# A gated linear recurrence feeding a multiplicative feed-forward layer: the decay parameter read as two rows, fewer turns on TensorE, and a new order of the steps

## The chip, the cores and the metric

The kernel runs on one core of a Trainium2 chip. The metric is device time in microseconds (us). The core has a matrix engine (TensorE, PE in the profile), a vector engine (VectorE, DVE), a scalar engine (ScalarE, ACT), a general engine (GpSimd, POOL) and a queue engine (SyncE, SP) that here only issues DMA transfers. Each engine works through its own list of instructions in order and waits on semaphores for the others.

## The reference, cut to what matters

```python
x, r_gate, i_gate: (4, 5824, 256)   a_param: (256,)
w1, w2: (256, 1024)   w3: (1024, 1024)   w_out: (1024, 256)

a_base = sigmoid(a_param)
log_a = 8 * sigmoid(r_gate) * log(clip(a_base, 1e-6, 1 - 1e-6))
a_t = exp(log_a)
x_gated = sqrt(maximum(1 - a_t * a_t, 1e-6)) * sigmoid(i_gate) * x
for t in range(5824):                    # each batch starts from h = 0
    h = a_t[:, t] * h + x_gated[:, t]
    y[:, t] = h
tokens = y.reshape(23296, 256)
out = (((tokens @ w1) * (tokens @ w2)) @ w3) @ w_out
```

## The kernel before

The 23,296 tokens are cut into 46 chunks, the first of 256 tokens and 45 of 512. Since nothing nonlinear stands between `w3` and `w_out`, their product `wp` is formed once at the start (the "fold": `Ft` turns a piece of w3, `Fc` copies it, `Fm` multiplies it with w_out, `Fe` evacuates it to `wp_sb`). Each chunk then goes through two halves.

*The recurrence.* `r`, `i`, `x` load the chunk with tokens on the partitions (L118). `R` and `I` are the tanh of the gates on ScalarE (L126, L136). `p` adds one to tanh(i) and `t` multiplies it with x, which gives `u` (L142, L146), mostly on GpSimd. `V` turns tanh(r) and `U` turns u so that channels lie on the partitions: either TensorE does it (`turn_pe`, L162, eight 128x128 transposes into PSUM) or a DMA transpose issued from SP (`turn_dma`, L174). The sets `TURN_R` and `TURN_U` say which chunks TensorE turns. A chunk that is in both sets is loaded with longer rows (`long_rows`, L109). `d` is the exponential that gives a_t, with the decay rate `la4` as scale and bias (L181), `s` its square, `q` the root on ScalarE, `g` the gated product on VectorE (L202), `h` the scan over time on VectorE, in two halves of 128 channels (L214), and `y` the cast to bf16 (L229).

*The feed-forward half.* `a` and `b` are the two up-projections, each in four groups of four matmuls into a tile of PSUM (L240; three such tiles); `c` copies the result of `a` to SBUF as bf16 (L256), `m` multiplies it with the result of `b` on VectorE (L262), `D` is the down-projection with `wp`, eight matmuls for 128 tokens (L269; two tiles of PSUM, which the turns share), `e` evacuates two of these (L281) and `o` stores 256 tokens (L294).

The decay rate is prepared once: `A0` and `A2` are short VectorE instructions on a tile of 128x2, and `A1` is an exponential on ScalarE between them (L349 to L366). `W` are matmuls on the identity whose result nobody reads; they stand ahead of the first work of TensorE.

The order isn't left to a scheduler. The program is recorded by walking a long string, `ORDER`, in which each word is one step with its chunk and part (`a12.3` is group 3 of `a` of chunk 12). Every engine's list has its instructions in the order of that string. Sets such as `DV_COPY`, `DV_EVAC`, `DV_SQUARE` and `DV_CAST` give the steps that VectorE takes; copies and evacuations not named there go to ScalarE, squares and casts not named there to GpSimd. `L` and `C` with a weight's name load a piece of a weight in f32 into a staging buffer and cast it to bf16. ScalarE has tanh and exp in one table and sqrt in another, so that each change between `R`, `I`, `d` and `q` brings a load of a table; copies work with either.

```python
nc.scalar.dma_start(out=la4, in_=a_param.rearrange("(cb p) -> p cb", p=P))
for word in ORDER.split():
    name, args = re.fullmatch(r"([LC]w[123o]\.|A\d\.|[A-Za-z]+)([\d.]*)", word).groups()
    steps[name](*(int(v) for v in args.split(".") if v))
```

Of the kernel before, what the change touches and what calls it, by code (L numbers as in the profile page):

```python
# [22 lines left out]
def kernel(  # L23
# [12 lines left out]
    nc = tc.nc  # L36
# [31 lines left out]
    la4 = consts.tile([P, NCB], F32, tag="la4")  # L68
    zz, zd, zt = (consts.tile([P, NCB], F32, name=tag, tag=tag) for tag in ("zz", "zd", "zt"))
# [9 lines left out]
    TURN_R = {0, 1, 2, 3, 4, 5, 7, 8, 13}  # L79
    TURN_U = {0, 1, 2, 3, 5, 8, 9}  # L80
    DV_TIMES = {0, 1, 2, 8}
    DV_PLUS = set()
    DV_HALF = set()
    DV_SQUARE = {(0, 0), (0, 1), (1, 0), (1, 1), (5, 0), (6, 0), (7, 1), (9, 1), (11, 0), (12, 0), (14, 0), (15, 1),
        (20, 1), (24, 1), (27, 0), (29, 0), (36, 0), (37, 0), (38, 0), (41, 0)}
    DV_CAST = {0, 20, 28, 37, 39, 40, 42, 45}
    DV_COPY = {(0, 3), (1, 1), (1, 3), (2, 1), (3, 2), (7, 2), (8, 0), (8, 1), (10, 0), (11, 1), (13, 0), (14, 0),
        (14, 2), (15, 3), (18, 1), (18, 3), (19, 3), (20, 3), (21, 3), (22, 3), (23, 1), (25, 0), (25, 2), (28, 1), (33,
        1), (33, 2), (36, 3), (40, 2), (41, 2), (41, 3), (44, 0), (45, 0)}
    DV_EVAC = {(0, 0), (1, 1), (2, 0), (2, 1), (3, 0), (4, 0), (4, 1), (5, 0), (6, 1), (7, 1), (8, 1), (9, 1), (10,  # L90
        0), (17, 0), (18, 1), (19, 0), (19, 1), (22, 0), (23, 1), (27, 0), (27, 1), (28, 1), (30, 0), (31, 0), (33, 1),
        (34, 1), (35, 0), (35, 1), (41, 1), (42, 0), (42, 1)}
    FOLD_ACT = {('c', 7), ('e', 0), ('e', 1), ('e', 4), ('e', 6), ('e', 7)}
    W_ACT = {('w2', 0), ('w3', 1), ('w3', 2), ('w3', 3)}
    W_DVE = {('w3', 0)}
    STAGE = {'w1': ['a', 'a'], 'w2': ['nrm', 'nrm'], 'wo': ['a', 'nrm'], 'w3': ['a', 'nrm', 'a', 'nrm', 'a', 'nrm',
        'a', 'nrm']}
    WARM = [30, 30, 24]
# [47 lines left out]
    def times(c, half):  # L146
# [168 lines left out]
    def load_w(nm, i):  # L315
        T["wf", nm, i] = held.tile([P, NCB, CT], F32, name="wf", tag=STAGE[nm][i])
        nc.sync.dma_start(out=staged(nm, i), in_=piece(nm, i)[0])
# [30 lines left out]

    def rates_abs():  # L349
        nc.vector.scalar_tensor_tensor(out=zz, in0=la4, scalar=-1.0, in1=la4, op0=ALU.mult, op1=ALU.min)  # L350
        nc.vector.tensor_scalar(la4, la4, -4.0, 0.0, op0=ALU.mult, op1=ALU.max)
# [22 lines left out]
    def last(c):  # L374
# [17 lines left out]
        "W": warm, "E": cast_ident, "A0.": rates_abs, "A1.": rates_exp, "A2.": rates,  # L392
# [3 lines left out]
        A0. r1 r0 i0 Lw3.0 x0 i1 A1. E R1 R0 x1 V0 V1 Lw1.1 Cw1.1 I0 A2. d0.0 d0.1 d1.0 d1.1 r2 Lw1.0 Lw2.0 Lw2.1 W1  # L396
        I1 s0.0 Cw3.0 s0.1 t0.1 s1.0 s1.1 W0 U0 i2 Cw1.0 q0 t1.1 g0 h0.0 q1 R2 U1 Lw3.1 h0.1 y0 W2 a0.2 g1 h1.0 c0.2
        V2 x2 h1.1 Lwo.1 Cw2.1 Cw2.0 Lwo.0 Ft0 a0.0 r4 a0.1 d2.0 c0.0 Lw3.2 c0.1 r3 b0.0 b0.1 s2.0 m0.0 m0.1 I2 d2.1
        Lw3.5 y1 Fc0 b0.2 b0.3 m0.2 s2.1 Lw3.4 a0.3 c0.3 m0.3 Cw3.1 Cwo.1 a1.2 Ft1 q2 a1.0 t2.1 Cwo.0 U2 i3 a1.1 c1.2
        b1.0 Fc1 c1.0 g2 c1.1 h2.0 R4 h2.1 m1.0 Lw3.3 Fm1 Fm0 Fe1 Fe0 y2 i4 b1.1 Cw3.5 r6 V4 b1.2 m1.1 m1.2 R3 V3 d4.0  # L400
        d4.1 a1.3 Ft5 d3.0 b1.3 a2.0 d3.1 Cw3.2 Fc5 x3 Ft2 c1.3 s4.0 Cw3.4 s4.1 I3 Lw3.6 Lw3.7 r5 s3.0 x4 s3.1 c2.0
# [127 lines left out]
```

## Time and profile before

| | |
|---|---|
| time, median of 3 runs | 521.2 us (521.09 to 521.59) |
| the profiled execution's own time | 520.88 us |
| its span, first to last instruction | 519.1 us |
| DMA: moved, mean rate | 123.28 MB, 237 GB/s |
| DMA transposes of u, of tanh(r) | 39, 37 |
| copies `c` of full chunks on ScalarE, on VectorE | 149 (mean 1012 ns), 31 (1214 ns) |
| evacuations `e` of 512 columns on ScalarE, on VectorE | 58 (mean 585 ns), 31 (680 ns) |
| table loads on ScalarE | 40 of 1283 ns |

The busy share of an engine is an average over the whole span. The matmuls overlap each other, so the mean duration of one (379 ns for 512 columns, 273 ns for 256) is more than the time from one start to the next (216 and 109 ns in an unbroken stream). ScalarE and VectorE overlap consecutive instructions a little as well. A wait is shown before the instruction that ended it, with what released it.

### The profile page before, as it was taken

What the parts mean: (1) busy time and instruction counts of PE and PEld (TensorE: products, weight loads), DVE (VectorE), ACT (ScalarE), POOL (GpSimd) and SP (SyncE); (2) the same over time, 40 slices, a digit from 0 to 9 for tenths busy, and PEclk for the clock granted to TensorE, in tenths of its full rate; (3) what the DMA queues carried; (4) which work ended last, traced back from release to release, by engine and by line L of the source; (5) the groups of instructions that cost most, each with busy time, mean ns of one, the idle gap of its engine ahead of it and who ended that gap; (6) DMA issues with size and microseconds to landing.
All of it is one profiled execution on the core that took longest, in us unless ns stands there. A gap on an engine that the chain in (4) does not pass through costs nothing.

```text
span 519.1 us, 8770 instructions
## 1 busy us (share of the span) xinstructions
PE 498.2 (96%) x3203; PEld 309.0 (60%) x3260; DVE 478.3 (92%) x456; ACT 429.7 (83%) x493; POOL 299.9 (58%) x251
## 2 busy tenths in 40 slices
PE   4799999999999999999999999999989999999997
PEld 4567656656565666566665655666556565666555
DVE  4999999999999999899999899999998998999973
ACT  6999998998898988999987997988977797766432
POOL 0668755786828674876566765756357746634000
PEclk9999999999999999999999999999999999999999
DMA  8999979899999786999989969988967988342113
GB/s 298 403 411 292 347 239 273 257 280 278 331 308 227 204 237 200 283 250 289 259 225 297 249 207 218 295 249 239 240 170 222 252 225 214 101 123 81 63 54 109
DMA packets 174604, 123.28 MB, mean 237 GB/s; under 512 B 84448, under 2 KB 170208, under 8 KB 174560
## 3 DMA queue, kind: packets, MB, share of 16 engines
q1 hardware_dynamic: 174288, 122.71, 83.8%
q8 instruction: 25, 0.41, 0.3%
q14 instruction: 19, 0.16, 0.1%
q10 hardware_dynamic: 272, 0.00, 0.0%
HBM read 78.91 MB, written 23.86 MB: 198 GB/s over the span
## 4 chain that ended last, share of the span: by engine, by line
PE 76%; DVE 16%; issue 5%; ACT 1%; DMA 1%; POOL 0%; DVEq 0%; ACTq 0%; POOLq 0%
PE pb L246 25%; PE po L277 24%; PE pa L246 23%; DVE g_t L266 6%; DVE h_t L225 4%; DVE sa L252 1%; PE pw L342 1%; DVE nrm L210 1%; PE ptr L167 1%; DMA la<-in_a_param_dram 1%; PE warm L238 1%; DVE nrm L195 1%; DVE nrm L207 1%; PE ptw L331 1%; DVE ot L252 1%
## 5 line engine op out<-in xcount | busy, mean ns | idle before, releaser
L246 PEld LDWEIGHTS <-w_sb 128*128 128x128 bf16 x1472 | 143.0, 98 | 150.8 <-issue 10.8
L266 DVE TENSOR_TENSOR g_t<-sa,pb 128x1024 bf16<-128x1024 bf16 (+1 forms) x184 | 215.9, 1199 | 17.4 <-PE pb L246 12.0
L254 ACT CAST sa<-pa 128x1024 bf16<-128x1024 f32 (+1 forms) x152 | 149.5, 1004 | 52.4 <-PE pa L246 47.2
L246 PE MATMUL pa<-y_t,w_sb 128*128 128x512 bf16 (+1 forms) x706 | 177.5, 377 | 5.0 <-DVE g_t L266 1.8
L246 PE MATMUL pb<-y_t,w_sb 128*128 128x512 bf16 (+1 forms) x709 | 177.9, 376 | 4.5 <-DVE sa L252 1.3
L277 PE MATMUL po<-wp_sb,g_t 128*128 128x256 bf16 x1456 | 179.4, 273 | 0.4
L277 PEld LDWEIGHTS <-g_t 128*128 128x128 bf16 x1456 | 142.3, 98 | 42.5
L225 DVE TENSOR_TENSOR_SCAN h_t<-a_t,h_t,nrm 128x512 f32<-128x512 f32 (+3 forms) x90 | 117.5, 1331 | 1.2
L160 POOL TENSOR_TENSOR u_t<-th_i,x_t 128x512 bf16<-128x512 f32 x84 | 113.8, 1373 | 1.6 <-DMA ut<-u_t 0.5
L233 POOL CAST y_t<-h_t 128x1024 bf16<-128x1024 f32 x38 | 44.5, 1170 | 118.1 <-DVE h_t L225 101.6
L195 POOL TENSOR_TENSOR nrm<-a_t 128x512 f32<-128x512 f32 x72 | 85.8, 1205 | 18.2 <-ACT a_t L188 18.1
L144 POOL TENSOR_SCALAR th_i<-th_i 128x1024 f32<-128x1024 f32 x42 | 48.7, 1163 | 30.7 <-ACT th_i L139 30.7
L188 ACT ACTIVATE a_t<-rt,la 128x512 f32<-128x512 bf16 x74 | 59.1, 818 | 3.0 <-DMA rt<-th_r 1.9
L139 ACT ACTIVATE th_i<-i_t 128x1024 f32<-128x1024 f32 (+1 forms) x46 | 48.3, 1051 | 7.1 <-DMA i_t<-in_i_gate_dram 4.2
L210 DVE SCALAR_TENSOR_TENSOR nrm<-nrm,ut 128x1024 f32<-128x1024 f32 x39 | 52.7, 1354 | 0.0
L254 ACT COPY ot<-po 128x512 f32<-128x512 f32 (+1 forms) x60 | 34.7, 578 | 17.0 <-PE po L277 16.2
L199 ACT ACTIVATE nrm<-nrm 128x1024 f32<-128x1024 f32 (+1 forms) x46 | 46.9, 1047 | 0.3
L252 DVE CAST sa<-pa 128x1024 bf16<-128x1024 f32 (+1 forms) x32 | 38.3, 1197 | 5.5 <-PE pa L246 5.4
L132 ACT ACTIVATE th_r<-r_t 128x1024 bf16<-128x1024 f32 x37 | 39.2, 1060 | 0.1
L199 ACT ACT_TABLE_LOAD x20 | 25.7, 1283 | 1.5 <-DVE nrm L195 1.1
L252 DVE COPY ot<-po 128x512 f32<-128x512 f32 (+1 forms) x33 | 21.9, 665 | 4.0 <-PE po L277 4.0
L195 DVE TENSOR_TENSOR nrm<-a_t 128x512 f32<-128x512 f32 (+1 forms) x20 | 18.2, 920 | 0.9 <-ACT a_t L188 0.9
(51 smaller groups left out, 155.0 us busy)
## 6 DMA issues: line engine op xcount, KB each, us to landing
r_t<-in_r_gate_dram SPq DMA_DIRECT2D x45, 512.0 KB, 5.5
i_t<-in_i_gate_dram SPq DMA_DIRECT2D x45, 512.0 KB, 5.2
x_t<-in_x_dram SPq DMA_DIRECT2D x45, 512.0 KB, 5.5
out_dram<-ot SPq DMA_DIRECT2D x89, 256.0 KB, 3.6
wf<-in_moe_w_dram SPq DMA_DIRECT2D x12, 512.0 KB, 8.9
wf<-in_moe_w_out_dram SPq DMA_DIRECT2D x2, 512.0 KB, 11.4
ut<-u_t SPq DMA_TRANSPOSE x39, 5.1
rt<-th_r SPq DMA_TRANSPOSE x37, 4.5
```

Source lines behind the costliest of these rows:

```text
L144: (nc.vector if c in DV_PLUS else nc.gpsimd).tensor_scalar(t, t, 1.0, 1.0, op0=ALU.add, op1=ALU.mult)
L160: (nc.vector if (c, half) in DV_HALF else nc.gpsimd).tensor_mul(out=u, in0=t, in1=xt)
L188: nc.scalar.activation(out=a, in_=pr, func=AF.Exp, scale=la4[:, cb:cb + 1], bias=la4[:, cb:cb + 1])
L195: eng.tensor_mul(out=T["n", c][:, cb, :w], in0=T["a", c][:, cb, :w], in1=T["a", c][:, cb, :w])
L199: nc.scalar.activation(out=T["n", c][:, :, :w], in_=T["n", c][:, :, :w], func=AF.Sqrt, scale=-1.0, bias=1.0)
L210: nc.vector.scalar_tensor_tensor(out=T["n", c][:, :, :w], in0=T["n", c][:, :, :w], scalar=1e-3, in1=T["pu", c][:, :, :w], op0=ALU.max, op1 ...
L225: nc.vector.tensor_tensor_scan(T["h", c][:, cb, lo:hi], T["a", c][:, cb, lo:hi], T["n", c][:, cb, lo:hi], init, ALU.mult, ALU.add)
L246: nc.tensor.matmul(out=pp[:, q, :w], lhsT=w_sb[:, cb, m * P:(m + 1) * P], rhs=T["y", c][:, cb, :w], start=(cb == 0), stop=(cb == NCB - 1))
L252: nc.vector.tensor_copy(out=dst, in_=src_ps)
L254: nc.scalar.copy(out=dst, in_=src_ps)
L266: nc.vector.tensor_mul(out=T["g", c][:, 2 * mp:2 * mp + 2, :w], in0=T["sa", c, mp][:, :, :w], in1=T["pb", c, mp][:, :, :w])
L277: nc.tensor.matmul(out=po, lhsT=T["g", c][:, k, j * P:(j + 1) * P], rhs=wp_sb[:, k, :], start=(k == 0), stop=(k == KD - 1), skip_group_che ...
```

## The change

The decay parameter is loaded as two rows of 128 values instead of 128 rows of two values. A new step, `A3`, turns it on TensorE into PSUM, and `A0` copies it to `la4` first. The sets that assign steps to engines are replaced, `times` works on one 128-channel half at a time for a fused chunk that TensorE doesn't turn (chunk 8), and `ORDER` is replaced as a whole. `CASTING` is empty, so the new branch in `load_w` does nothing.

```diff
+    la_rows = consts.tile([NCB, P], F32, tag="la_rows")
...
-    TURN_R = {0, 1, 2, 3, 4, 5, 7, 8, 13}
-    TURN_U = {0, 1, 2, 3, 5, 8, 9}
+    TURN_R = {0, 1, 2, 3, 4, 9, 16}
+    TURN_U = {0, 1, 2}
     DV_TIMES = {0, 1, 2, 8}
-    DV_PLUS = set()
-    DV_HALF = set()
-    DV_SQUARE = {(0, 0), (0, 1), (1, 0), (1, 1), (5, 0), (6, 0), (7, 1), (9, 1), (11, 0), (12, 0), (14, 0), (15, 1),
-        (20, 1), (24, 1), (27, 0), (29, 0), (36, 0), (37, 0), (38, 0), (41, 0)}
-    DV_CAST = {0, 20, 28, 37, 39, 40, 42, 45}
-    DV_COPY = {(0, 3), (1, 1), (1, 3), (2, 1), (3, 2), (7, 2), (8, 0), (8, 1), (10, 0), (11, 1), (13, 0), (14, 0),
...
-    DV_EVAC = {(0, 0), (1, 1), (2, 0), (2, 1), (3, 0), (4, 0), (4, 1), (5, 0), (6, 1), (7, 1), (8, 1), (9, 1), (10,
...
+    DV_PLUS = {6, 10}
+    DV_HALF = {(3, 0), (4, 0), (6, 1), (7, 0), (10, 1), (12, 0), (13, 0)}
+    DV_SQUARE = {(0, 0), (0, 1), (1, 1), (4, 0), (5, 0), (7, 0), (10, 1), (13, 0)}
+    DV_CAST = {1, 4, 9, 11}
+    DV_COPY = {(0, 2), (2, 0), (3, 2), (3, 3), (4, 0), (4, 1), (6, 1), (8, 0)}
+    DV_EVAC = {(9, 0), (9, 1)}
+    FOLD_ACT = {('c', 6), ('e', 1), ('e', 2), ('e', 3), ('e', 5), ('e', 6), ('e', 7)}
+    W_ACT = {('w2', 0), ('w2', 1), ('w3', 4)}
+    W_DVE = {('w1', 0), ('w3', 1)}
...
+    def rates_turn():
+        pt = psum.tile([P, 2, CT], F32, name="pr_la", tag="pab")
+        nc.tensor.matmul(out=pt[:, 0, :NCB], lhsT=la_rows, rhs=ident_f[:NCB, :NCB], is_transpose=True,
+                         start=True, stop=True)
+        T["la"] = pt[:, 0, :NCB]
+
     def rates_abs():
+        nc.vector.tensor_copy(out=la4, in_=T["la"])
...
     ORDER = """
-        A0. r1 r0 i0 Lw3.0 x0 i1 A1. E R1 R0 x1 V0 V1 Lw1.1 Cw1.1 I0 A2. d0.0 d0.1 d1.0 d1.1 r2 Lw1.0 Lw2.0 Lw2.1 W1
-        I1 s0.0 Cw3.0 s0.1 t0.1 s1.0 s1.1 W0 U0 i2 Cw1.0 q0 t1.1 g0 h0.0 q1 R2 U1 Lw3.1 h0.1 y0 W2 a0.2 g1 h1.0 c0.2
...
-        e44.1 D45.1 o44.1 e45.0 o45.0 D45.2 e45.1 o45.1 D45.3 e45.2 o45.2 e45.3 o45.3
+        r1 E A3. A0. A1. A2. R1 r0 R0 V1 d1.0 d1.1 i0 V0 x0 s1.0 I0 i1 W0 Lw1.0 t0.1 s1.1 W2 d0.0 d0.1 x1 I1 Cw1.0
+        s0.0 s0.1 q0 t1.1 q1 Lw1.1 r2 Cw1.1 R2 Lw2.1 Lw2.0 W1 U0 g0 h0.0 h0.1 y0 U1 Lw3.1 i2 Cw2.1 a0.0 a0.3 a0.1 V2
...
+        e44.0 e44.1 o44.0 D45.0 e45.0 o44.1 D45.1 e45.1 o45.1 o45.0 D45.2 D45.3 e45.2 e45.3 o45.3 o45.2
         """
 
-    nc.scalar.dma_start(out=la4, in_=a_param.rearrange("(cb p) -> p cb", p=P))
+    nc.scalar.dma_start(out=la_rows, in_=a_param.rearrange("(cb p) -> cb p", p=P))
```

## The prediction

> **What bounds the kernel now.** I first read busy shares and the chain that ended last.
>
> ```profile
> PE 498.2 (96%) x3203; PEld 309.0 (60%) x3260; DVE 478.3 (92%) x456; ACT 429.7 (83%) x493; POOL 299.9 (58%) x251
> PE 76%; DVE 16%; issue 5%; ACT 1%; DMA 1%; POOL 0%; DVEq 0%; ACTq 0%; POOLq 0%
> ```
>
> TensorE (PE) has 96% and carries 76% of the chain; VectorE (DVE), the next busiest, carries 16%. So PE's instruction stream sets the end, and VectorE interrupts it. The question is where PE isn't working. The table by stages, cut at the first up-projection (17.4 us) and at the first down-projection (50.7 us), answers:
>
> ```profile
> 0.00:17.40 17.40, 8.15 (x109) 8.01 (x110) 9.83 (x27) 11.98 (x15) 3.21 (x8) 1.00 0.88 327
> 17.40:50.70 33.30, 31.55 (x268) 21.63 (x274) 31.96 (x38) 32.56 (x40) 24.38 (x22) 1.00 1.07 371
> 50.70:150.00 99.30, 98.12 (x631) 60.61 (x641) 96.99 (x94) 92.02 (x104) 67.89 (x57) 1.00 0.99 288
> 150.00:300.00 150.00, 148.85 (x904) 89.74 (x920) 143.56 (x129) 136.63 (x157) 100.00 (x83) 1.00 0.95 249
> 300.00:450.00 150.00, 145.95 (x882) 87.69 (x898) 140.68 (x123) 123.70 (x143) 89.42 (x72) 1.00 0.85 223
> 450.00:519.10 69.10, 65.56 (x418) 41.28 (x422) 55.32 (x50) 32.85 (x39) 14.98 (x12) 1.00 0.28 85
> ```
>
> Columns: length, then busy time of PE, PEld, DVE, ACT, POOL, granted clock, DMA share, GB/s. From 17.4 to 450 us PE is idle for 1.75 + 1.18 + 1.15 + 4.05 = 8.1 us. Up to 150 us ScalarE (ACT), VectorE and the DMA engines are all nearly full too. After the last matmul (515.9 us) come 3.2 us of copy, store and closing. An edit therefore pays by taking instructions out of PE's stream, by starting it earlier, or from those 8.1 us.
>
> The timeline shows what holds the start:
>
> ```profile
> 0.73 0.45 ACTq L497 DMA_DIRECT2D la<-in_a_param_dram  x1
> 5.67 0.16 DVE L350 SCALAR_TENSOR_TENSOR zz<-la 128x2 f32<-128x2 f32 x1 [5.67 <-DMA la<-in_a_param_dram]
> 5.97 1.56 ACT L130 ACTIVATE th_r<-r_t 128x1024 bf16<-128x1024 f32 x2
> 8.84 4.86 PE L238 MATMUL warm<-ident 128*128 128x128 bf16 x60
> 13.53 0.83 PE L167 MATMUL ptr<-ident,u_t 128*128 128x128 bf16 x12
> 17.37 0.60 PE L246 MATMUL pa<-y_t,w_sb 128*128 128x256 bf16 x4 [1.67 <-DVE y_t L233]
> ```
>
> The decay parameter lands 4.9 us after its issue; ScalarE's exponential stands before its first tanh and waits for it. But the turn of u at 13.53 stands behind 60 warm-up matmuls, so two things hold the first `a`.
>
> **What the Trainium skill says.** "DMA: Bandwidth & Descriptors", Specifications, puts full rate at transfers of 512 B or more. The old load is 256 packets of 4 B (trace: first at 2.83 us, last at 4.88, landed 5.64); the new one is 2 rows of 512 B. "TensorE: Matmul & The Clock Gate", Back-to-back issue gap, gives N/2.4 + 2.5 ns warm: 56 ns for 128 columns. The trace agrees: eight turns take 0.61 us with a 0.219 us last one, (0.61 - 0.219)/7 = 0.056. "ScalarE: Activation LUTs", What ACT_TABLE_LOAD costs, has 1.28 us and a drain of 1.38 for each switch; here the next instruction starts 1.294 us after the load (load at 11.66, Sqrt at 12.95), so I use 1.294. "SBUF — State Buffer", SBUF: two separate sides, says that VectorE and GpSimd lock a shared port: here VectorE's gated product averages 1.354 us with both inputs in SBUF against 1.207 for the one of its shape that reads u from PSUM.
>
> **The change part by part.**
>
> *Turns.* TURN_R goes from 9 chunks to 7, TURN_U from 7 to 3: 6 turns of 8 transposes leave PE, all after the first `a`: 48 x 0.056 = -2.7 us of PE's stream. Nothing hides these, since PE is the bound. The turn of the parameter adds one matmul before PE has other work; behind its wait stand only the turns of chunk 1, which need the later r tile. The six become DMA transposes: 1,024 packets of 256 B at 24 ns on 16 engines = 1.5 us of DMA each, and about 1.4 us of SyncE's (SP's) time to issue. Chunks 3, 5 and 8 also lose the long-row loading. A DMA turn waits on SP for GpSimd's product, and behind it stand the next loads of r, i and x, which ScalarE's tanh needs. This costs nothing while u lands before its use; the rival prices the other case.
>
> *Start.* Two rows should land about 3.6 us (first old packet 2.83 plus the old 0.76 from last packet to landing). Transpose, copy and exponential then end near 4.7. The first r tile has landed by then (0.74 + the shortest r landing, 4.0), so the first tanh moves from 5.97 to about 4.8: -1.2 us on ScalarE. The new order puts all 84 warm-up matmuls before the turn of chunk 0's u, not 60. PE starts near 5.9 instead of 7.58, but 24 more at 0.06 us give 1.4 us of the 1.7 back. I take -0.4 for the first `a`, with -1.2 and +0.9 as bounds: the first if ScalarE's lead decides how soon the folds end, the second if u of chunk 3, now a DMA transpose behind 16 loads and all 14 weight pieces, is late for `a3`, which stands before the first `D` now. For u3: 30 transfers x 1.36 + its own 1.5, + 1.8 start + 2 landing = 46.1 us; product, scan and cast follow in 4.7 (50.8), then three groups of `a3` (2.6), where the old kernel began `D` at 50.7.
>
> *Copies and evacuations.* 24 copies and 29 evacuations move from VectorE to ScalarE. ScalarE gains 24 x 0.905 + 29 x 0.466 = +35.2 us (start to start; alone 1.012 and 0.585), but the order has 32 table loads instead of 40: -10.4. Sum near 455 us, 88% of the span. Per chunk: copies 3.6, evacuations 0.9, two tanh 1.9, two exponentials 1.4, a root 0.95, tables 0.9, or 9.7 us against PE's 32 x 0.216 + 32 x 0.109 = 10.4. It still fits beneath PE. VectorE loses 24 x 1.13 + 29 x 0.60 = 44.5 us, and 12 squares (7) and four casts (2.5) go to GpSimd (POOL); seven half-products and two additions come back (about +6). It drops to near 430, GpSimd rises to some 310. Cost at nothing: PE hides it. If it doesn't, the copy of `a` queued behind a root and its table load is what PE meets.
>
> *Order.* The trace of before can't show the new one's stalls. Bounds: -4 (half of the 8.1 us go, as VectorE's share of the chain does) and +6 (below). I take 0: VectorE has more room after 150 us, the middle of the first 100 us has less.
>
> *Tail.* The last two stores are swapped: o45.3, which waits for ScalarE's last copy, stands before o45.2 in SP's queue, so another issue follows it: +0.35 us.
>
> Sum: -2.7 - 0.4 + 0 + 0.35 = -2.75. The profiled execution took 520.88 us (span 519.10 and 1.78 around it), 0.3 below the median: 518.1 there, **518.4** as a median.
>
> **Rivals.**
>
> *Late u (slower).* Place: chunks 5 to 8. Up to U8 the new order issues 39 loads and 14 weight pieces (53 x 1.36 us, 512 KB at the 385 GB/s of loads alone), 12 transposes (1.5) and 6 stores (0.7): 94 us of DMA, against 34, 14, 7 and 5 at the same step before (79 us). From 1.8 us on and with 2.5 us to land, u8 is there at 98.6; product, scan and cast make y8 at 103.3. PE's work before `a8` (58 groups of up-projection at 0.865, 23 `D` at 0.87, folds and turns 12.8) sums to 83.0; from 17.0 and with 2.3 us of idle it arrives at 102.3. So the margin is about -1 even if DMA never pauses. For it: the old u7 comes out by this sum at 79.4, its issue was at 77.3. Against it: transposes may overlap loads (packet times run above the share 1.0), worth 3 to 4 us. Each pause of SP, which waits in order, adds its length to PE. It decides once pauses exceed about 3 us; with 5 to 8 us of them the stall is 4 to 6: 523.5.
>
> *Stalls fall too.* VectorE carries 16% of the chain and loses a tenth of its work; the idle stage 300 to 450 us holds chain pieces of VectorE. Half of the 8.1 us gone, less a little: 515.3. Against it: PE's waits are short and scattered, and each copy that leaves VectorE joins ScalarE's queue.
>
> *Exchange.* The turns' 2.7 us leave PE and come back as waits of 2 to 3 us at `a3` to `a8`: 521.0, no change.
>
> That the new load lands no earlier than the old is small: the first `a` stays and the result is 518.8, inside the first case.
>
> **How the numbers follow.** Likeliest, 0.48; stalls fall too 0.12; exchange 0.14; late u 0.26. The likeliest's own range is 516.5 to 520.3. For eight in ten the range takes most of late u and of the falling stalls: 515.3 to 524.0. What a measurement of this kernel can tell from no change is about 0.2%, 1.04 us. Faster: the second case and nearly all of the first (0.46) = 0.58. Same: exchange and the rest = 0.16. Slower: late u = 0.26.
>
> **What would show it.** Right: 120 - 48 = 72 `ptr` matmuls, first tanh near 4.8 us, first `pa` near 17, 32 table loads, ScalarE near 455 us, PE idle near 8 us after the start. Wrong: first `D` after 52 us, a gap of PE at chunk 5 to 8 released by u's product or scan, or ScalarE the owner of a good part of the chain. If PE's idle time past 50 us doubles, the forecast is wrong by as much.

## The result: no change that can be told, with a stream on TensorE that is 2.7 us shorter

| | before | changed |
|---|---|---|
| time, median | 521.22 us (521.09 to 521.59, 4 runs) | 521.68 us (520.63 to 522.32, 4 runs) |
| ratio, 95% interval | | 1.0006 [0.9985, 1.0026] |
| the profiled execution, its span | 520.88, 519.1 us | 522.25, 520.5 us |

The forecast was 518.4 us. The busy shares and the chain that ended last, after the change:

```profile
PE 498.5 (96%) x3157; PEld 308.1 (59%) x3213; DVE 437.3 (84%) x395; ACT 454.1 (87%) x538; POOL 310.3 (60%) x258
...
PE 71%; DVE 9%; ACT 9%; issue 5%; DMA 5%; SPq 1%; DVEq 0%; ACTq 0%
```

The work moved as planned: VectorE lost 41 us, ScalarE gained 24, GpSimd 10. But PE's share of the chain fell from 76% to 71%, and ScalarE and DMA transfers, 1% each before, carry 9 and 5%. The stages, with the columns of the earlier table (length, busy PE, PEld, DVE, ACT, POOL, granted clock, DMA share, GB/s):

```profile
0.00:17.40 17.40, 10.11 (x120) 9.82 (x121) 10.20 (x28) 13.17 (x17) 3.39 (x9) 1.00 0.90 336
17.40:50.70 33.30, 29.84 (x238) 20.34 (x241) 32.52 (x37) 30.93 (x37) 21.55 (x19) 0.95 1.01 341
50.70:150.00 99.30, 95.50 (x583) 56.82 (x593) 94.44 (x86) 93.98 (x114) 58.66 (x47) 1.00 1.01 281
150.00:300.00 150.00, 146.81 (x899) 89.30 (x914) 129.85 (x105) 139.28 (x165) 105.63 (x85) 1.00 0.97 261
300.00:450.00 150.00, 149.10 (x900) 89.48 (x915) 122.73 (x103) 137.59 (x161) 99.85 (x83) 1.00 0.89 226
450.00:520.50 70.50, 67.09 (x429) 42.37 (x433) 47.54 (x40) 39.17 (x49) 21.24 (x18) 1.00 0.29 96
```

Three rows are to be compared with those of before. From 50.7 to 150 us PE is idle for 3.8 us instead of 1.2, and VectorE is hardly relieved there: 94.4 us instead of 97.0. From 150 to 300 us VectorE has 14 us less to do, and PE is still idle for 3.2 us instead of 1.15. From 300 to 450 us VectorE has 18 us less, and PE is idle for 0.9 us instead of 4.05. So the change gained time only in the last of these stages, and lost it in the two ahead of it; less work on VectorE alone doesn't decide.

Busy time is a rough measure of PE, since its ends are modelled. A sharper one is PE's *lag*: the time at which a down-projection starts, less the PE work that stands ahead of it in the kernel's list (0.864 us for a group of `a` or `b`, 0.872 for a `D` or an `Fm`, 0.446 for a turn or an `Ft`, from the unbroken streams, and half of it for the groups and turns of the short chunk; warm-ups and the turns of the first two chunks count as nothing). Lag grows only where PE waits or runs slowly. It is my own sum from the trace and the list of steps:

| kernel (profiled execution) | PE work | lag at D1.0 (some 50 us) | D12.1 (170) | D23.1 (286) | last D |
|---|---|---|---|---|---|
| before | 489.1 | 20.2 | 21.9 | 22.6 | 26.7 |
| changed | 486.4 | 22.1 | 27.4 | 30.4 | 30.9 |

The account of the profiled executions closes: 2.7 us less work, +1.9 of lag at D1.0, +3.6 from there to D12.1, +2.3 to D23.1, -3.6 from D23.1 to the end, -0.1 behind the last `D`: +1.4 us, and the two executions differ by 522.25 - 520.88 = 1.37.

*The start* went better than forecast for ScalarE and for the first `a`. From the timeline of the changed kernel:

```profile
0.73 0.53 ACTq L510 DMA_DIRECT2D la_rows<-in_a_param_dram  x1
2.22 0.23 PE L357 MATMUL pr_la<-ident_f,la_rows 2*128 2x2 f32 x1 [2.22 <-DMA la_rows<-in_a_param_dram]
4.08 1.57 ACT L127 ACTIVATE th_r<-r_t 128x1024 bf16<-128x1024 f32 x2 [1.00 <-DMA r_t<-in_r_gate_dram]
16.25 1.69 PE L246 MATMUL pa<-y_t,w_sb 128*128 128x256 bf16 x12 [2.33 <-POOL y_t L233]
```

The two rows land 1.5 us after their issue instead of 4.9. The first tanh now waits for its own r tile (4.08 instead of 5.97), and the first `a` comes at 16.25 instead of 17.37. But the first `D` comes at 54.3 instead of 50.7. Of these 3.6 us, 1.7 are more PE work ahead of it in the new order. The other 1.9, and the 1.1 us that the first `a` had won, went in part to more waits between the first `a` and the first `D`, and for the greater part to the clock that was granted to PE right after its wait for the first `a`:

```profile
17.00:18.00 1.00, 1.00 (x10) 0.83 (x9) 1.00 (x2) 1.00 (x2) 0.00 (x0) 0.68 1.03 418
18.00:19.00 1.00, 1.00 (x10) 0.84 (x8) 1.00 (x1) 1.00 (x3) 0.00 (x0) 0.50 1.01 405
19.00:20.00 1.00, 1.00 (x7) 0.67 (x6) 0.97 (x3) 1.00 (x3) 0.00 (x0) 0.50 1.03 382
20.00:21.00 1.00, 1.00 (x7) 0.74 (x6) 1.00 (x3) 1.00 (x3) 0.58 (x1) 0.61 1.10 418
```

The third column from the right is the clock: half speed for some 3.4 us, which costs 1.7.

*From 50 to 132 us* PE's waits are short and many. From its timeline in that stretch:

```profile
64.17 0.62 PE L167 MATMUL ptr<-ident,th_r 128*128 128x128 bf16 x8 [1.04 <-ACT th_r L127]
86.13 0.82 PE L246 MATMUL pa<-y_t,w_sb 128*128 128x512 bf16 x3 [0.49 <-DVE g_t L266]
87.26 1.02 PE L246 MATMUL pa<-y_t,w_sb 128*128 128x512 bf16 x4 [0.30 <-DVE g_t L266]
98.68 1.90 PE L246 MATMUL pa<-y_t,w_sb 128*128 128x512 bf16 x8 [0.18 <-POOL y_t L233]
119.59 1.04 PE L246 MATMUL pa<-y_t,w_sb 128*128 128x512 bf16 x4 [0.40 <-DVE y_t L233]
```

Each bracket holds the wait and what ended it: ScalarE once, VectorE's products and casts, GpSimd's cast. No single one is large. Behind them stand further waits; between 53 and 132 us the chain of waits of the changed kernel names PE for 12% only (three lines), and DMA transfers of x (9.1%) for the first time:

```profile
by line: issue 19.4%; DVE g_t L266 16.4%; ACT sa L254 10.2%; DMA x_t<-in_x_dram 9.1%; PE pa L246 6.3%; DVE sa L252 5.9%; ACT ot L254 3.8%; ACT a_t L188 3.6%; PE po L277 3.3%; ACT th_r L129 3.3%; DVE nrm L210 2.9%; PE pb L246 2.2%; SPq L118 
```

In the same stretch of the kernel before, three PE lines alone carried 41%:

```profile
by line: DVE g_t L266 20.9%; PE po L277 17.9%; PE pb L246 12.9%; issue 12.7%; PE pa L246 10.5%; DVE h_t L225 8.7%; DVE nrm L195 4.4%; DVE sa L252 4.3%; DVE nrm L207 3.0%; PE ptr L167 1.7%; DVE ot L252 1.7%; DVE nrm L210 1.5%; DVEq L252 0.1%
```

*From 170 to 289 us* (D12.1 to D23.1) the lag grows by 3.0 us, and two waits for ScalarE's copies of `a`, near 272 and 279 us, hold 2.0 of them. At the second, the copy stands behind a table load and a root:

```profile
275.98 1.28 ACT L199 ACT_TABLE_LOAD   x1
277.27 1.06 ACT L199 ACTIVATE nrm<-nrm 128x1024 f32<-128x1024 f32 x1
278.24 0.99 ACT L254 CAST sa<-pa 128x1024 bf16<-128x1024 f32 x1
279.28 1.02 PE L246 MATMUL pb<-y_t,w_sb 128*128 128x512 bf16 x4 [1.24 <-ACT sa L254]
```

No experiment below takes these two up.

### The profile page after: what moved, and what is told of

It is laid out like the page before. It is cut to its first block, busy times and chain, and to the rows that moved or that the text cites. A ratio compares the mean times of both kernels' runs of the same rounds, so it can differ in the third digit from the quotient of the medians.

```text
span 520.5 us, 8667 instructions
## 1 busy us (share of the span) xinstructions
PE 498.5 (96%) x3157; PEld 308.1 (59%) x3213; DVE 437.3 (84%) x395; ACT 454.1 (87%) x538; POOL 310.3 (60%) x258
## 4 chain that ended last, share of the span: by engine, by line
PE 71%; DVE 9%; ACT 9%; issue 5%; DMA 5%; SPq 1%; DVEq 0%; ACTq 0%
PE po L277 23%; PE pb L246 22%; PE pa L246 22%; DVE g_t L266 4%; ACT sa L254 3%; DMA rt<-th_r 3%; DMA x_t<-in_x_dram 1%; PE warm L238 1%; PE pw L348 1%; ACT th_r L129 1%; DVE sa L252 1%; ACT ot L254 1%; DVE h_t L225 1%; DVE nrm L210 1%; ACT nrm L199 1%
## 5 line engine op out<-in xcount | busy, mean ns | idle before, releaser
L254 ACT CAST sa<-pa 128x1024 bf16<-128x1024 f32 (+1 forms) x176 | 173.4, 1005 | 38.9 <-PE pa L246 33.0
L233 POOL CAST y_t<-h_t 128x1024 bf16<-128x1024 f32 (+1 forms) x42 | 49.3, 1174 | 124.6 <-DVE h_t L225 118.7
L225 DVE TENSOR_TENSOR_SCAN h_t<-a_t,h_t,nrm 128x512 f32<-128x512 f32 (+3 forms) x90 | 121.0, 1373 | 1.5
L195 POOL TENSOR_TENSOR nrm<-a_t 128x512 f32<-128x512 f32 x84 | 96.6, 1167 | 23.3 <-ACT a_t L188 23.3
L210 DVE SCALAR_TENSOR_TENSOR nrm<-nrm,ut 128x1024 f32<-128x1024 f32 x43 | 60.7, 1413 | 6.0 <-DMA ut<-u_t 2.5
L188 ACT ACTIVATE a_t<-rt,la 128x512 f32<-128x512 bf16 x78 | 62.5, 820 | 2.5 <-DMA rt<-th_r 2.4
L141 POOL TENSOR_SCALAR th_i<-th_i 128x1024 f32<-128x1024 f32 x40 | 45.7, 1144 | 28.6 <-ACT th_i L136 28.4
L254 ACT COPY ot<-po 128x512 f32<-128x512 f32 (+1 forms) x89 | 51.6, 584 | 11.5 <-PE po L277 11.0
L199 ACT ACT_TABLE_LOAD x16 | 20.5, 1283 | 0.3
L188 ACT ACTIVATE a_t<-ptr,la 128x512 f32<-128x512 bf16 (+1 forms) x14 | 9.9, 751 | 1.4 <-PE ptr L167 1.4
L252 DVE CAST sa<-pa 128x1024 bf16<-128x1024 f32 (+1 forms) x8 | 9.2, 1148 | 1.4 <-PE pa L246 1.4
L157 DVE SCALAR_TENSOR_TENSOR u_t<-th_i,x_t 128x512 bf16<-128x512 f32 (+1 forms) x5 | 6.0, 1217 | 3.2 <-ACT th_i L136 3.0
```

The lines of the kernel that those rows point to most:

```text
L188: nc.scalar.activation(out=a, in_=pr, func=AF.Exp, scale=la4[:, cb:cb + 1], bias=la4[:, cb:cb + 1])
L195: eng.tensor_mul(out=T["n", c][:, cb, :w], in0=T["a", c][:, cb, :w], in1=T["a", c][:, cb, :w])
L199: nc.scalar.activation(out=T["n", c][:, :, :w], in_=T["n", c][:, :, :w], func=AF.Sqrt, scale=-1.0, bias=1.0)
L210: nc.vector.scalar_tensor_tensor(out=T["n", c][:, :, :w], in0=T["n", c][:, :, :w], scalar=1e-3, in1=T["pu", c][:, :, :w], op0=ALU.max, op1 ...
L225: nc.vector.tensor_tensor_scan(T["h", c][:, cb, lo:hi], T["a", c][:, cb, lo:hi], T["n", c][:, cb, lo:hi], init, ALU.mult, ALU.add)
L233: eng.tensor_copy(out=T["y", c][:, :, :w], in_=T["h", c][:, :, :w])
```

## The experiments

My theory after the result: the rows gain what was forecast or more, the new assignments gain after 300 us, and the turns' 2.7 us were exchanged for waits between 50 and 300 us, because PE isn't what that stage waits for in the new order. Rivals: one part of the change is bad by itself (the rows, the DMA turns, the copies); the DMA engines or SP's queue are full; VectorE or a few misplaced steps hold PE. Ratios are to the kernel before, measured beside each run on the same chip (medians there 521.1 to 521.7 us).

### One part at a time in the old order

**Rows alone** (`b_rows`): the old order and sets, with the parameter as rows.

```diff
-        A0. r1 r0 i0 Lw3.0 x0 i1 A1. E R1 R0
+        E A3. A0. r1 r0 i0 Lw3.0 x0 i1 A1. R1 R0
-    nc.scalar.dma_start(out=la4, in_=a_param.rearrange("(cb p) -> p cb", p=P))
+    nc.scalar.dma_start(out=la_rows, in_=a_param.rearrange("(cb p) -> cb p", p=P))
```

> The kernel before, with the decay parameter read as two rows and turned on TensorE, and nothing else (the identity's cast and the new step stand first in the order). If the wait for the parameter is what holds the start: first tanh near 4.1 us instead of 5.97, first up-projection near 16.3 instead of 17.4, time 520.2 (-1.0). If the warm-up matmuls ahead of the turn of u hold it: first tanh near 4.1 but first up-projection within 0.4 us of before, time 520.8 to 521.3.

Measured: 519.99 us, ratio 0.9967 [0.9946, 0.9988]. The lag at D1.0 is 18.3 instead of 20.2; at the last `D` it is still 1.0 lower (25.7). The first `a` comes at 15.84 us instead of 17.37. The load of the parameter did hold the start, and this part gains 1.3 us.

**DMA turns alone** (`b_turns`): the new `TURN` sets in the old order, each new DMA turn issued behind the step that produces its input, and the product of chunk 8 in two halves as in the change.

```diff
-    TURN_R = {0, 1, 2, 3, 4, 5, 7, 8, 13}
-    TURN_U = {0, 1, 2, 3, 5, 8, 9}
+    TURN_R = {0, 1, 2, 3, 4, 9, 16}
+    TURN_U = {0, 1, 2}
-        e1.1 s6.0 c4.0 b4.0 s6.1 U5 s7.1
+        U5 e1.1 s6.0 c4.0 b4.0 s6.1 s7.1
```

> The kernel before with the new sets of turns alone (48 transposes fewer on TensorE, six more DMA transposes, chunks 3, 5 and 8 without long rows); the words of the turns that move to DMA stand directly after their producers. If late u eats the gain: TensorE's lag behind its own work grows by 3 to 6 us between 50 and 150 us (1.6 before), time 521.5 to 525. If the turns are harmless and the new order is at fault: that growth stays under 2.5 us and the time is 518.5 to 519.5.

Measured: 549.19 us, ratio 1.0515 [1.0475, 1.0555], far outside both forecasts. The waits between 75 and 125 us show why. First SP's own queue, then ScalarE (waited for, us in total, times, longest):

```profile
SPq L180 <- ACT th_i L139: 11.3, 1, 11.3
SPq L180 <- DVE u_t L160: 7.2, 1, 7.2
```

```profile
ACT th_i L139 <- DMA i_t<-in_i_gate_dram: 6.7, 1, 6.7
```

L180 is the DMA turn. SP waits in order, so a turn that can't start holds every load behind it. The wait of 7.2 us, to 97.7 us, is U8's for its product; the load of i10 goes out after it, and ScalarE waits 6.7 us for that tile. The wait of 11.3 us, to 120.4 us, is V13's. Its input is done at 115.8 us; the rest of the wait is for one of the two `rt` tiles, the one that V11 filled, and the last instruction that reads that tile (`d11.1`) ends at 120.35 us. PE's lag grows by 27 us from D1.0 to D8.0 (157 us); some 8.5 of them are a clock of 0.50 behind PE's waits, for 17 us in all. My placement, not the turn, is what this prices: it shows only that a DMA turn cannot be put where I put it.

**Copies and evacuations alone** (`b_copies`): the new `DV_COPY` and `DV_EVAC` in the old order.

> The kernel before with the new sets for the copies and evacuations alone (24 copies and 29 evacuations to ScalarE), the order unchanged. With 40 table loads ScalarE gets 35 us more and is near 465 us busy. If ScalarE's load is what costs the middle of the changed kernel: 524 or more, with lag growing by more than 6 us from 50 to 300 us (2.3 before). If VectorE was the source of the stalls from 300 to 425 us: growth there falls from 4.1 to under 1.5 us and the time is 518 to 520.

Measured: 548.75 us, ratio 1.0513 [1.0487, 1.0539]. The lag grows from 22.4 us at D1.0 to 47.2 at D23.1, so the first case came in, and by far more than it asked for. ScalarE is busy for 465 us, 85% of the span, so it isn't full. From 100 to 350 us VectorE waits for ScalarE's copies; in the kernel before no such line is among the ten largest waits of that stretch:

```profile
DVE g_t L262 <- ACT sa L250: 27.4, 13, 5.4
```

My reading, which no run tests further, is that the copies stand behind other ScalarE steps in a list that was written for fewer. Neither piece gains anything alone, in the places that I gave them in the old order: sets and order are made for each other, and a sum of parts, as I made it, has no parts to add.

### Single suspects in the new order

**The first wait of PE** (`a_warm`): 30 of the 84 warm-ups moved behind U1, into the 2.3 us in which PE waited for the first `a`.

> The changed kernel with one word moved: the second group of 30 warm-up matmuls stands after the turn of chunk 1's u, directly before the first up-projection. If the idle stretch of 2.3 us before the first up-projection lets the granted clock fall to half for about 3 us: clock 1.00 throughout, all runs at 519.3 to 520.3 instead of 520.6 to 522.3 (median -1.5 to -2). If the clock is chance and the start is bound by the recurrence: first up-projection within 0.3 us of 16.25 and the median within 0.5 us of 521.7.

Measured: ratio 1.0005 [0.9993, 1.0016], 521.83 us of 20 runs. In the profile the clock stays at 1.00 and the lag at D1.0 falls from 22.1 to 20.4, and it ends at 29.7. The median is no lower than the 521.68 of the changed kernel's four runs, so the half clock isn't what made the result. With the same rows and the full clock, the first `a` comes at 15.59 us in this order and at 15.84 in the old one (`b_rows`), yet the lag at D1.0 is 20.4 here and 18.3 there. So the new order loses some 2 us already between the first `a` and the first `D`. The later runs are edits of this kernel.

**The rows undone** (`a_la`): the parameter loaded as before, `A3` taken out.

> The changed kernel with the warm-up group moved and the decay parameter loaded as before, 256 packets of 4 bytes, no turn. If the two rows' gain is real in this order too: first tanh near 6.0 instead of 4.1 us, lag at the first down-projection 21.5 to 22.5 instead of 20.4, time +1.2 to +2. If something later takes it up: time within 0.4.

Measured: 524.12 us, ratio 1.0044 [1.003, 1.0058], lag at D1.0 +2.6. The rows are worth about 2 us in the new order (2.3 by the medians, 524.12 - 521.83; 2.0 by the ratios). They aren't the loss.

**Four turns back on PE** (`a_turns`): U3, U8, U9 and V8 just ahead of their use.

```diff
-    TURN_R = {0, 1, 2, 3, 4, 9, 16}
-    TURN_U = {0, 1, 2}
+    TURN_R = {0, 1, 2, 3, 4, 8, 9, 16}
+    TURN_U = {0, 1, 2, 3, 8, 9}
```

> The changed kernel with the warm-up group moved, and four turns back on TensorE: u of chunks 3, 8 and 9 and tanh(r) of chunk 8 (chunks 3 and 8 load long rows again; chunk 8's u is one VectorE instruction again). TensorE's own work +1.8 us. If late u or the DMA load is what costs the middle: the lag's growth from 50 to 150 us falls from 5.7 to under 3, and the time is 520 or less. If VectorE and ScalarE are what is short there: growth stays over 4.5 and the time is 522.5 to 524.

Measured: 530.59 us, ratio 1.0172 [1.015, 1.0194]. Turns at 0.446 us each explain 1.8 of the 8.8 us that it is above `a_warm`. Another 3.8 us stand in the lag at D1.0 already (24.2 instead of 20.4). A step of 4.3 us in the lag, at 120 us, is the largest; ahead of that the chain runs from U8's turn (109.9 us) over gated product, scans and products on VectorE to the `pa` matmuls at 115.8; 1.7 of the 4.3 us are a clock of 0.50 from 116 to 119.4 us. Where a turn stands in PE's list decides when VectorE may go on. A price of the turns doesn't come out of this run.

**Chunk 8's product** (`a_t8`): x8 loaded ahead of x9, and the product of chunk 8, which stood ahead of three products of `m` on VectorE, moved behind them.

> The changed kernel with the warm-up group moved, and two words moved more: x of chunk 8 is loaded before x of chunk 9, and chunk 8's u on VectorE stands after the products of chunk 5 instead of ahead of them. If VectorE's wait at the head of its queue (for x, then 2.1 us of u in two halves) holds TensorE near 86 us: the step of +0.93 us of lag there goes, growth from 50 to 150 us falls to about 4.5, time -0.5 to -1. If the stretch is bound by VectorE's sum of work, the step comes back within 20 us and the time is unchanged within 0.3.

**VectorE's extra steps back on GpSimd** (`a_pool`): `DV_PLUS` and `DV_HALF` emptied.

> The changed kernel with the warm-up group moved, and the seven half-products and two additions of i that the change gave VectorE given back to GpSimd (about 8 us less on VectorE, 11 more on GpSimd, all before 130 us). If VectorE, 94% busy between 50 and 150 us, is the limit there: growth falls from 5.7 to under 4, time -1.5 to -2.5. If ScalarE or the loads are: growth within 1 of 5.7; if GpSimd makes u late: growth over 7.

**V9 later** (`a_v9`): the turn that waited for ScalarE at 62 us (64 in the changed kernel), moved behind D2.0 and a3.3.

> The kernel a_warm with one step moved: TensorE turns tanh(r) of chunk 9 (V9) after D2.0 and a3.3 instead of ahead of them, where it waited 0.8 us for ScalarE at 62 us. Theory (the stalls of the changed order between 50 and 150 us are single steps placed ahead of their producers, and each can be taken out by itself): the step of 1.0 us in PE's lag at 62 us goes, the lag at D5.0 is 23.0 instead of 23.9, and the time falls by about 0.9 from a_warm's 521.8. Rival (PE runs behind what ScalarE and VectorE finish, so a wait that is taken away returns at the next dependent step): the lag at D5.0 stays within 0.4 of 23.9 and the time within 0.4 of 521.8.

Measured: `a_t8` 523.86 us, 1.0044 [1.0023, 1.0066]; `a_pool` 523.24, 1.0034 [1.0018, 1.005]; `a_v9` 522.23, 1.0014 [0.9994, 1.0033]. In `a_t8` the step of 0.9 us in the lag at 86 us is gone, and 4.2 us come by 93 and 2.1 more by 98 us. PE's timeline shows of what:

```profile
85.06 1.04 PE L277 MATMUL po<-wp_sb,g_t 128*128 128x256 bf16 x8
...
88.67 1.02 PE L246 MATMUL pb<-y_t,w_sb 128*128 128x512 bf16 x4 [1.71 <-DVE sa L252]
91.11 1.86 PE L246 MATMUL pb<-y_t,w_sb 128*128 128x512 bf16 x4 [1.41 <-ACT sa L254]
92.77 1.91 PE L277 MATMUL po<-wp_sb,g_t 128*128 128x256 bf16 x8
```

Two waits for copies of `a` (`sa`), 3.1 us together, and behind them the same eight `po` matmuls take 1.91 us instead of 1.04: the granted clock is 0.50 from 90.2 to 97 us, which adds some 3 us to the work that PE does in it. In `a_v9` the step at 62 us is gone, 0.9 come at 74, and the lag at D5.0 is 24.4 against 23.9. So these two waits, taken away, came back at later steps. VectorE with 2.1 us less to do between 50.7 and 150 us (91.4 us, `a_pool`) doesn't help either: the lag grows by 5.2 us from D1.0 to D12.1 instead of 5.7, and it starts 1.7 higher. Neither of the two steps is the cause by itself. VectorE's sum of work doesn't look like the limit, but `a_pool` gave that work to GpSimd, which also feeds PE, so the run doesn't rule it out.

**Fewer transfers** (`a_nostore`): the stores of chunks 0 to 7 left out.

> The kernel a_warm without the stores of chunks 0 to 7, so that part of the output is not written: about 3.9 MB, some 10 us less of DMA work between 50 and 150 us, where the DMA share is 1.00. If the transfers are what PE waits for in the first 150 us (ScalarE and VectorE waiting for late r, i and x, and these for the DMA engines), the lag grows by less than 3 us from D1.0 to D12.1 instead of 5.7, and the time falls to 518 to 519.5. If the waits come from the order in which ScalarE, VectorE and PE do the steps that depend on each other, the growth stays above 4.5 and the time within 0.7 us of 521.8.

Measured: 520.63 us, ratio 0.9977 [0.9962, 0.9992]. The lag grows by 4.0 us from D1.0 to D12.1: neither the 3 of one theory nor the 4.5 of the other, and the time lies between theirs too. Those transfers, with SP's waits for them, are some 1.7 of the 5.7 us, and the rest stays without them.

**Loads ahead of turns, turns ahead of loads** (`a_loads`, `a_early`): only SP's list is changed. In the first, ten loads of r, i and x go one place ahead, before the DMA turn that stood before them; in the second, ten turns go ahead of the load before them, each still behind the step that makes its input.

```diff
a_loads:
-        r7 ... V6 ... U4 ... r5 ... i5 ... V7 ... x5
+        r7 ... V6 ... r5 ... U4 ... i5 ... x5 ... V7
a_early:
-        r7 ... V6 ... U4 ... r5 ... i5 ... V7 ... x5
+        V6 ... U4 ... r7 ... r5 ... V7 ... i5 ... x5
```

> The kernel a_warm with ten loads of r, i and x between chunk 5 and chunk 19 issued one place earlier in SP's list, ahead of the DMA turn that stood before them; nothing else moves. Between 40 and 150 us SP waits for 38 us at DMA turns in a_warm and for only 2 us for a free buffer at a load, while in the order before with rows it waits for 31 and 16: there the loads run ahead until buffers are full, here they come when SP gets to them. Theory (SP's waits at turns make the loads late, and these the tanhs and all that follows): the lag grows by at most 4.5 us from D1.0 to D12.1 instead of 5.7, and the time falls by 1 us or more below 521.8. Rival (the recurrences are late for reasons other than the loads): the growth stays within 0.6 of 5.7 and the time within 0.7 of 521.8, or the turns, now behind a load, come later and it is slower.

> The mirror of the run in which ten loads went ahead of turns (that one: 523.1 us, lag growth 8.2 instead of 5.7 from D1.0 to D12.1). Here ten DMA turns (V5, V6, V7, U4, U5, U6, U8, V15, U12, U13) are issued one place earlier, ahead of the load that stood before them, each still behind the step that makes its input; nothing else moves. Theory (what the stage follows is when the turns land): the growth falls below 5.2 and the time by 0.5 us or more below 521.8. Rival (SP then stands longer at the turns and the loads behind come late, so that a place gained by one is lost by the other): growth 5.5 or more, time 521.5 or more.

Measured: `a_loads` 523.12 us, ratio 1.0037 [1.0025, 1.0049], lag growth from D1.0 to D12.1 8.2; `a_early` 526.01 us, ratio 1.0092 [1.0061, 1.0123], growth 7.6 (1.7 of it a clock of 0.50 from 55.5 to 58.9 us) and 2.1 more at D1.0, where PE waits 2.4 us for the fold's last pieces from ScalarE. Both theories fell, and both directions are worse, as the rivals had it. ScalarE's waits between 40 and 150 us say what happened (waited for, us in total, times, longest), first in `a_warm`:

```profile
ACT th_r L129 <- DMA r_t<-in_r_gate_dram: 2.6, 2, 1.5
...
ACT a_t L188 <- DMA rt<-th_r: 0.9, 2, 0.7
```

With the loads ahead:

```profile
ACT a_t L188 <- DMA rt<-th_r: 6.3, 3, 3.3
...
ACT th_r L129 <- DMA r_t<-in_r_gate_dram: 0.9, 1, 0.9
```

With the turns ahead:

```profile
ACT th_r L129 <- DMA r_t<-in_r_gate_dram: 6.7, 3, 3.4
...
ACT a_t L188 <- DMA rt<-th_r: 0.6, 1, 0.6
```

Ten places won by the loads are lost by the turns (`rt`), and the other way round: ScalarE then waits some 4 us more for whichever comes late. So in the new order loads and turns share one queue, and what one gains the other loses, on ScalarE's path. Whether SP's waiting in order or the DMA engines, busy all through the stage in both orders (share 1.00 in `a_warm`, 0.99 in the kernel before), leave no room, these runs don't tell; `a_nostore` gives the engines a part. `b_rows` has 6 DMA turns fewer to fit in, and its SP even stands at loads for a free buffer (16 us between 40 and 150 us, against 2 in `a_warm`): there the loads run ahead.

### Is PE's time worth anything in that stage?

**2.7 us of PE's time put back** (`a_extra`, and `b_extra` on `b_rows` as the control):

```diff
         pp = psum.tile([P, 2, CT], F32, name=nm, tag="pab")
+        if nm == "pa" and 3 <= c <= 8 and ("extra", c) not in T:
+            T["extra", c] = True
+            for _ in range(8):
+                nc.tensor.matmul(out=pp[:, 0, :P], lhsT=ident, rhs=ident, start=True, stop=True)
```

> The kernel a_warm with 8 extra matmuls of 128 columns (0.446 us) ahead of the first up-projection of each of the chunks 3 to 8, 2.7 us of PE's time in all, as much as the six turns that the change took out of PE's list; their result is overwritten. Theory (exchange: in this stage PE waits for other engines, so PE's time was not what the end depended on, and taking 2.7 us out of it could bring nothing): at least 1.5 of the 2.7 us are swallowed by waits, and the time is at most 523.0. Rival (PE is the bound here too and its waits come on top): 524.2 to 524.8.

> The control for the run with extra matmuls: the kernel before with the parameter as two rows, and the same 2.7 us of extra matmuls at the same chunks. In this order PE waits for only 1.8 us between 50 and 150 us, so both theories expect most of the 2.7 us to be added: 522.2 to 522.9 against 520.0 without them. If it adds less than 1.5 us here as well, PE's own time is not the bound of that stage in either order, and the 2.7 us of the turns were never to be had.

Measured: `b_extra` 522.87 us, ratio 1.0021 [1.0003, 1.0038] against `b_rows`' 0.9967: +2.8 us, give or take 1.4 by the two intervals. `a_extra` 522.93, ratio 1.0015 [0.9998, 1.0033] against `a_warm`'s 1.0005: +0.5 us, give or take 1.1 (+1.1 by the medians). The profiles show where it goes (lag, with the extra matmuls counted as no work; "first extra" is the lag ahead of the first of them):

| | first extra | D1.0 | D8.0 | D12.1 | last D | profiled time |
|---|---|---|---|---|---|---|
| b_rows | 18.3 | 18.3 | 20.4 | 20.5 | 25.7 | 519.95 |
| b_extra | 19.2 | 19.2 | 22.5 | 22.7 | 28.6 | 523.15 |
| a_warm | 20.4 | 20.4 | 26.1 | 26.1 | 29.7 | 521.02 |
| a_extra | 20.6 | 21.1 | 26.4 | 26.4 | 30.1 | 521.42 |

In the old order the lag is 0.9 higher ahead of the first extra matmul already, which these can't have caused. Counted from there, the same 2.7 us at the same chunks cost 1.2 us by D8.0 and 2.0 by the last `D` in the old order, and 0.1 and 0.2 in the new one. The stage from 50.7 to 150 us, first `a_warm`, then `a_extra`:

```profile
50.70:150.00 99.30, 95.49 (x583) 56.92 (x593) 93.55 (x85) 93.72 (x114) 57.46 (x46) 1.00 1.00 285
```

```profile
50.70:150.00 99.30, 97.80 (x637) 59.48 (x635) 95.27 (x85) 94.00 (x113) 57.69 (x46) 1.00 1.03 278
```

PE (first number after the length) is busy for 2.3 us more in the same stretch: the extra work went into its waits. The same two rows of the old order, `b_rows` and `b_extra`:

```profile
50.70:150.00 99.30, 97.75 (x623) 59.70 (x632) 96.08 (x94) 91.55 (x104) 66.22 (x55) 1.00 1.01 288
```

```profile
50.70:150.00 99.30, 99.01 (x675) 61.64 (x673) 95.98 (x92) 90.84 (x102) 64.78 (x55) 1.00 1.01 286
```

There PE had 1.5 us of waits to fill, and it fills 1.3. That is the exchange, shown from the other side: PE's time in that stage is worth nearly nothing in the new order. In the old one it is worth about half its price by D8.0, three quarters at the end, and all of it by the times.

### Halves of the two orders joined

The two orders meet: at D23.1 (near 284 us) all but two steps that the changed order has done are done in the old one too. `h23` takes the old order and sets, with rows, up to D23.1, and the changed order and sets for the steps left; `h27` joins at D27.0; `r20` is the reverse, the changed order up to D20.2 and the old one behind it.

> This kernel takes the order and the assignments of the kernel before (with the parameter as two rows) up to the down-projection D23.1, near 284 us, and those of the changed kernel for every step that is left. Theory (each order loses its time in its own place: the changed order in the first 300 us, the order before after 300 us): PE's lag behind its own work is 21.2 us at D23.1 in the kernel before with rows, and the changed kernel adds only 1.0 us from there to the end where the order before adds 4.6. So the lag ends near 22.2 and the time near 516.4 us, 3.5 under the rows alone. Rival (the late part of the changed order runs well only because its first half arrives later, with engines further ahead, so that the two halves cannot be cut apart): the lag grows by 3 or more again after D23.1 and the time is 519 to 522.

> The same with the cut at D27.0, near 328 us, where the order before has already done every step that the changed order has done (and 30 more). Theory: the step of 1.0 us near 313 us of the order before stays in (lag 22.7 at the cut), so the lag ends near 23.7 and the time near 517.9 us, about 1.5 above the cut at D23.1. Rival (halves that cannot be cut apart): 519 to 522, as with the other cut.

> The reverse: the changed order and assignments (with the first weights' cast moved, as in the run called a_warm) up to D20.2, near 266 us, then those of the kernel before. Theory: the lag is 26.2 us at the cut and grows by the 4.4 us that the order before adds from there, so it ends near 30.6 against 29.7: 522.7 us, about 1 above a_warm, although the steps of 2.4 us that the changed order has at 271 and 278 us are gone. If it comes out at 520 or below, the late part of the order before is not what costs it 4 us, and it was what it inherited from its own first half.

| | time, runs | ratio | lag D1.0 | D23.1 | last D |
|---|---|---|---|---|---|
| b_rows | 519.99 (6) | 0.9967 [0.9946, 0.9988] | 18.3 | 21.2 | 25.7 |
| h23 | 518.38 (18) | 0.9947 [0.9931, 0.9962] | 18.4 | 20.8 | 23.6 |
| h27 | 519.80 (15) | 0.9963 [0.995, 0.9976] | 20.2 | 22.6 | 25.6 |
| a_warm | 521.83 (20) | 1.0005 [0.9993, 1.0016] | 20.4 | 28.6 | 29.7 |
| r20 | 527.00 (5) | 1.0093 [1.0063, 1.0123] | 20.4 | 29.6 | 33.8 |

`h23` beats both kernels, by 0.5%; the rows alone bring 0.3% of it, and its interval overlaps that of `b_rows`, so the times don't show that the join gains. The profiles do, in one execution each: the lag grows by 2.8 us behind the join, where the old order adds 4.6 and I expected 1.0. So the late half of the changed order seems to gain when it is put behind the old first half, but about half of what I took from its own trace. `h27` grows by 3.0 from D23.1, like `h23`; it began with half a clock (0.50 from 17.5 to 20.9 us; lag 1.8 higher at D1.0 than `h23`, whose list is the same up to there), and the intervals of the two overlap, so I can't put one join above the other. `r20` is worse than expected: 6.9 us more lag from D20.2 (26.8) to the end, against 4.4. `h23` and `r20` point one way: the old order is the better one early, the new one late. For `h23` the stage from 300 to 450 us reads:

```profile
300.00:450.00 150.00, 149.29 (x910) 88.69 (x908) 125.26 (x104) 136.14 (x160) 96.13 (x78) 1.00 0.85 229
```

PE is idle for 0.7 us there, with VectorE at 125 us; in the kernel before it was 4.05 with VectorE at 141.

## Why the prediction was wrong, by its own steps

- *Turns, -2.7 us.* Here it failed. The count was right (72 turns, 48 fewer), and the work left PE's list. "Nothing hides these, since PE is the bound" is largely true of the order whose profile I read (`b_extra`: +2.8 us of time for 2.7 of work), but the change brought another order, and in that one PE isn't the bound between 50 and 150 us (`a_extra`: 0.1 us of lag by D8.0, +0.5 of time). I priced an instruction of the new kernel with the bound of the old one.
- *Order, 0 with bounds -4 and +6.* This is the term that was mis-sized, the same failure seen from the other side. With the rows and the full clock in both (`a_warm` against `b_rows`), the new order and sets cost 2.1 us of lag up to D1.0, 3.5 more to D12.1 and 1.9 more to D23.1, and win back 3.6 behind it: +3.9 us in all, against 2.7 us of work saved. The value lies inside my bounds, but I took 0 where the profile of before showed ScalarE, VectorE and DMA nearly full up to 150 us. I had noted "the middle of the first 100 us has less" and priced it at nothing.
- *Start, -0.4 for the first `a`.* That the parameter held the start was right; the size was too small: -1.1 at the first `a`, -1.3 us of the whole in the old order, about -2 in the new. The rows landed at 2.2 us, not 3.6, and PE's first turn came at 5.20 us, not 5.9; but the 84 warm-ups took 6.6 us where 60 had taken 4.7, so that 24 more cost 1.9 us, not 1.4 (some 38 of them came 107 ns apart and only the rest 56). It is luck that these two errors cancel in the turn of chunk 0's u, 0.44 us earlier as forecast; the other 0.7 us come from a shorter chain behind it (3.16 us instead of 3.84 from that turn to the first `a`). That PE's pause behind the warm-ups could halve its clock I hadn't thought of. My sign for trouble, a first `D` after 52 us, came (54.3), for that clock, for 1.7 us more PE work ahead of it and for waits behind the first `a`, not for a late u3.
- *Copies and evacuations, nothing.* The amounts held (454 us on ScalarE, 437 on VectorE, 310 on GpSimd, 32 table loads). The price of nothing did not: near 272 and 279 us PE waits for ScalarE's copies, 2.0 us of lag, the second time for a copy behind a root and its table load, just where I had said that PE would meet it. After D23.1 the lag grows by 0.5 us instead of 4.1: there the stalls did fall, as the rival "stalls fall too" had it. `b_copies` (+27 us) shows that the sets alone don't bring this.
- *Tail, +0.35.* Not seen: the time from the last `D` to the end of the span is 4.1 us, against 4.2.
- *Rivals.* "Exchange" (14%) came in by its number (521.0 forecast, 521.68 measured) and by its mechanism between 50 and 150 us (`a_extra`). The number is in part luck: that rival knew nothing of the 2.0 us at the copies, nor of the 3.6 us won behind D23.1. The places agree only in part: of the waits between D1.0 and D12.1 some 2 us stand at `a` and `b` of chunks 5 to 7, none at `a3` and `a4`, 1.2 us at V9 and most of the rest at chunks 9 and 10. "Late u" was right in one point: loads behind DMA turns in SP's one queue are scarce in that stage (`a_loads`, `a_early`). But it isn't u that comes late for PE, it is r and the turned tanh(r) for ScalarE, from chunk 5 on, and it did not cost 4 to 6 us more.

What is shown: between 50 and 150 us of the new order PE's own time has nearly no price, leaving out 3.9 MB of stores brings 1.7 us of lag, and moving ten places in SP's queue costs time either way. The two single steps that I moved gave nothing. What is argued only: that the six added DMA turns are what filled the queue. Taking four of the PE turns back (`a_turns`) brought stalls of its own, so that step isn't proved, nor how the lag of 5.7 us is shared among the queue, the DMA engines, ScalarE and VectorE.

## What to carry to other kernels

Before you count an instruction that leaves the busiest engine as gained, ask whether that engine still is the bound in the stage *after* the change; the cheapest test is to put the same amount of dead work back and see whether the time takes notice. An assignment of steps to engines and the order of the steps are one design: put singly into the old order, parts of a change that is neutral as a whole cost 27 and 28 us here. Where two orders lose in different places, look for a step at which both have done the same work, and try the better halves joined; here that may have brought 1 to 2 us beyond the rows.

## What the runs showed that I had not expected

- A wait of PE can cost more than its length. In 7 of the 19 profiled executions the granted clock fell to 0.50 for some 3.4 us, or a multiple of that, behind gaps of 1.8 us or more between two matmuls' starts (2.54 us in the changed kernel, 2.10 in `a_turns`, 2.28 in `a_early`, 2.09 and 1.79 in `a_t8`, 1.76 in `h27`): 1.7 us on top for each 3.4. But gaps of 2.36 us (`a_loads`, 62 us), 2.41 (`r20`, 273), 2.48 (`a_v9`, 10) and 2.90 (`b_copies`, 264) went by at full clock. The Trainium skill, "TensorE: Matmul & The Clock Gate", Part 1, says that activity is judged in free-running windows of about 3.4 us; the length agrees, and executions of the same list do differ (`h23` and `h27` up to D1.0), but gaps well below a window sufficed here, where the page's table asks for a whole idle one. In the tables the clock of the first stretch reads 1.00, but its records begin only at some 10 us: up to 10.5 us the 128-column matmuls of the changed kernel come 107 ns apart, after that 56.
- A DMA turn in front of SP's queue that can't start yet costs every load behind it, and its input isn't all that it may wait for: in `b_turns` one stood for 11.3 us, the last 4.6 of them for a free tile to write to.
- The parameter as two rows landed in 1.5 us instead of 4.9 us for 256 packets of 4 B.
- Single executions of one kernel spread by 3 to 5 us here (`h23` 516.89 to 520.98). Differences of 1 us between two edits need some 15 runs each, by the intervals here. PE's lag in a trace shows more, since steps come back at the same place in several kernels (those near 272 and 280 us in the changed kernel, `a_t8` and `a_v9`), but it too starts differently from one execution to the next: the same list gave 18.3, 18.4 and 19.2 us at D1.0 at full clock (`b_rows`, `h23`, `b_extra`).
